# The MLP's second layer norm as a factor per token behind its first product

## The chip, the cores and the metric

The kernel runs on one core of one Trainium2 chip. Its time is the device time of one launch in microseconds (us), as the median over runs: 713.09 us of three runs (712.26 to 713.43). The core has five engines that matter here, each with its own instruction queue that it works through in order: PE (matrix products; PEld is its weight load), DVE (elementwise work and reductions), ACT (functions with scale and bias), POOL (elementwise work, on-chip memory alone) and SP (issues DMAs). Products land in eight PSUM banks, which PE shares out among all its jobs. Every wait is a semaphore, so an instruction that waits holds back all that stands behind it in its queue.

## The reference

```
xn = layernorm(x)                                  # x: 2048 tokens x 512, eps 1e-5, no weights
out = x + A(xn) + B(xn)
A:  q, k, v = xn@wq, xn@wk, xn@wv                  # 32 heads of 16; 4 segments of 512 tokens
    per segment: causal softmax attention, mixed by sigmoid(beta) with
    a linear memory  phi(q)M / (phi(q)z + 1e-6),  phi(t) = t+1 if t>0 else exp(t)
    then M += phi(k)^T v,  z += sum phi(k)
    A = o @ wo
B:  y = layernorm(xn)                              # a second norm of tokens already normalized
    h = gelu(y @ w1 + b1)                          # 512 -> 1792, tanh form
    B = h @ w2 + b2
```

The mean of a normalized token is zero, so the second norm only scales it: y = xn * r with one number r per token, where r = 1/sqrt(v/(v+eps) + eps) for a token of variance v.

## The kernel before

All products but the softmax-weighted sum over V and some small ones are made of two-part f16 numbers: each operand is split into a high and a low half, and three matmuls (high by high, high by low, low by high) stand for one. `split3` (L456 on, its matmul on L465) issues these: 12 matmuls for a 512-long contraction.

Tokens arrive as [128, 512] tiles `xt`. `norm_stats` takes mean and variance on DVE (L397, L398), adds eps, goes through Ln and Exp on ACT, and refines with a Newton step on DVE (L407 to L410). It makes two pairs of factor and offset per token: one for the first norm, one for both norms in one. `norm_apply` applies a pair in place, on POOL (L418). `ln_tr` transposes a normalized tile with four PE transposes (L450), and ACT (L453) and DVE (L454) write its high and low halves.

This is done twice. The kind "X" loads tokens, takes statistics, applies the first pair and fills `xnT`, the transposed tokens of a segment of 512, which feed Q, K and V (`qk_proj`, `v_nat`). The kind "Y" loads the same tokens again, applies the second pair, and fills `yT`, half a segment of 256 tokens, which feeds the MLP. Either has one buffer, which is refilled when its last reader is done.

The MLP runs in 16 units j: half segment j//2, and one half of the 1792 features (7 tiles of 128). Unit j has seven D steps (`d_jobs`): 12 matmuls of 256 columns each into a bank, evicted with scale `CG` and bias `b1t` into `hz`, four of the seven by ACT (L724), three by DVE (L726), as `Z_ON` says. G (`gelu`, L731) is one ACT instruction over all seven, 1792 columns, behind a load of the gelu table; the next exponential loads the other table back (L850). H (`h_split`) splits the result on POOL and ACT (L738 to L740), and e (`e_part`, L764) multiplies by w2 in two accumulator banks. `hz` is the memory of `hT`, two buffers, one for each feature half.

Attention runs in 16 groups i of 8 heads, four for each segment: T makes Q (or K) and sends it through DRAM into stacked form (`qst`, `kst`); M makes the logits once to find row maxima (DVE, L597, with a read of the result after each); R transposes the maxima and sends them through DRAM into `qst`; S makes the logits again and takes exponentials (ACT, L635), with the causal mask on POOL (L644); pv sums over V (L659); O divides (DVE, ACT and POOL); Z, Qd and Q are the memory part; N and K update it; out is the last product (L783). A DVE copy of one number (`fence`, L767) stands in the middle of each MLP unit's second product.

The order of all work is written out in a string, `ORDER`: each letter takes the next step of one of some thirty streams, and all engines get their instructions in that one order. `BANKS` gives the PSUM bank of each product in turn. Fourteen `warm` steps of eight idle matmuls each (L796) can be put anywhere; before, all stand in the start.

Of the kernel before, what the change touches and what calls it, by code (L numbers as in the profile page):

```python
# [9 lines left out]
F32 = mybir.dt.float32  # L10
# [40 lines left out]
Z_ON = "AVAVAVA"  # L51
# [6 lines left out]
def streams():  # L58
# [23 lines left out]
    for n in range(2 * NSEG):  # L82
        again += [("Y", n, 0, 0), ("Y", n, 0, 2), ("Yt", n, 0, 0), ("Yt", n, 0, 1)]
# [21 lines left out]
    "aacttuttcacutvaatcvucuevaatevaacvccvutbcbwtccvtbvvcwfvwtdcvttxxextxvwyxbchxgxxyxoowxoyxowowvyoyzoyzniiibccyygpz"  # L105
    "iiccniipznzyiyfzAnsqpiioiqizzmAqqiwpAzhoAoiiqqzzjpocjiqijjqizjoAjoBAiikskkAkjqiqjqmjjisqjiojiqbiskkkpkibbplafoA"
    "oAjpgjloojqjqjqjlohakkkpkojiqiAajsoijijqjiqjmiAiAifippBkkqqBikipqikoqilBsgaoplahqjjqlqqqjqjoBoijqiajqipamkkkksa"
    "ioojpiqjqiqijqjiaaqjqjsbmqiqBiiBfoikkkbBpkbibpghopoolqqpjqojjjloojiqjqiqilmkpkkkijojiqqqijjqijqiqjqiipkkkpkbiif"
    "mnillnglnnrjjrjqiirpjiqjisqijqikkmkkjijrjjioijioijikkpkkhilmfolomjjbgojqqjpljqjoobsmbkkkkjqqisjqqjijqiqjiqijoiq"
    "iiskkmippqiqpiskaklmiohlfoiqpqaqamqgploooaomjqjqqjqmjqaojpqpsiiqiqoioiqjpqiqiikkkkoapjiqijqijqjpqiqjqsjaqaoihkk"  # L110
    "kkaalmoqjjlbfobqjqjlsqmjgbbqjkkmmkkjqjqmojjjohiojiikkkkipiifplilonnliiiniipmripgnojjmjrjsjorijibkkkpkmiiqjqjqij"
    "qqiijsqiqjohjqiiqpqiipmkpkkskrillfmmlogqqbjjoojqjqjjoomkkpkkiijhooiqjiqjqijqiqpsjiqqjibbpqiqipkkkkliiqaslfoioom"
    "papqqqamgpooasjqqjqjmaoojqjlqjqiqiapqikmkikkiqipoiqjqjaoohijqjaqiqiisopaojiqqjiakmspkkklbopfjqlbqjmjgqjjqqjqlob"
    "bkkkmkmjqjqqiqjqijqjqoimijkpkkkliilfnimiiplgnniipirmoiorponijpjobojjioisjqqjpiiqkkkkiiprijsqsqjiqqjjimqqijrijkk"
    "ipkbsklfloqjqmjglojjqqqjjomsokkkkopjmioiijojqijqipqjqjqiiqqiikppkkkliqlfbbqliqqqimoipmgooojpjqqjojjoomjiikkkpki"
    "qijqijqjqiijqjiqjqiikisqpiskkkqpioqplooplqjjqqjjojjqlopkkkkjqjqqjjojqjoqqpspqkkkkqpqqlqqpqqmpqqqqqqqqqqqmqllqqr"
    "rrr"
# [33 lines left out]
def infini_mixer_kernel(ctx: ExitStack, tc: tile.TileContext, x, wq, wk, wv, wo, beta, w1, b1, w2, b2, out):  # L151
# [68 lines left out]
    def col(j):  # L220
        return sc[:, j:j + 1]
# [166 lines left out]
    stats = cst.tile([P, S // P, 2, 2], F32, name="stats")  # L388

    def norm_stats(tok, tiles):  # L390
# [21 lines left out]
    def norm_apply(tok, tiles, twice, act):  # L412
        for j, t in enumerate(tiles):
            a, b = stats[:, tok + j, twice, 0:1], stats[:, tok + j, twice, 1:2]
# [7 lines left out]
    def ln(kind, n, b, part):  # L422

        tok = 4 * n + 2 * b if kind == "X" else 2 * n
        if part == 0:
            lt[kind, n, b] = ts = []
            for j in range(2):
                name = ("nN", "nD")[j] if (kind, n, b) == ("X", 0, 1) else "xt"
# [3 lines left out]
        elif part == 1:  # L432
            norm_stats(tok, lt[kind, n, b] + (lt[kind, 0, 1] if n == 0 else []))
        else:
            norm_apply(tok, lt[kind, n, b], kind == "Y", (kind, n, b) == ("X", 0, 1))

    def ln_out(kind, n, b, k):
        if kind == "X":
            if n not in xnT:
                xnT[n] = sb.tile([P, KT, 2, SEG], F16, name="xnT")  # L440
# [439 lines left out]
```

## Time and profile before

| | |
|---|---|
| median of 3 runs | 713.09 us (712.26 to 713.43) |
| the profiled execution | 712.69 us, span of its instructions 711.0 us |
| granted TensorE clock | 0.998 |
| PE busy | 693.3 us, 98% |
| PEld busy | 392.6 us, 55% |
| ACT busy | 535.9 us, 75% |
| DVE busy | 531.8 us, 75% |
| POOL busy | 363.7 us, 51% |

The span runs from the first to the last instruction. Busy shares are averages over three stages that differ: a start, in which weights arrive and are split; a long middle, in which attention and MLP units are interleaved; an end, in which no more maxima are to be found and the last unit and group are finished. Matmuls overlap in the pipeline and their ends are modelled, so that PE counts as busy in short waits too. The chain that ended last, followed back from the last instruction, tells in which stage which engine sets the pace.

### The profile page before, as it was taken

What the parts mean: (1) busy time and instruction counts of PE and PEld (TensorE: products, weight loads), DVE (VectorE), ACT (ScalarE), POOL (GpSimd) and SP (SyncE); (2) the same over time, 40 slices, a digit from 0 to 9 for tenths busy, and PEclk for the clock granted to TensorE, in tenths of its full rate; (3) what the DMA queues carried; (4) which work ended last, traced back from release to release, by engine and by line L of the source; (5) the groups of instructions that cost most, each with busy time, mean ns of one, the idle gap of its engine ahead of it and who ended that gap; (6) DMA issues with size and microseconds to landing.
All of it is one profiled execution on the core that took longest, in us unless ns stands there. A gap on an engine that the chain in (4) does not pass through costs nothing.

```text
span 711.0 us, 16718 instructions
## 1 busy us (share of the span) xinstructions
PE 693.3 (98%) x6261; PEld 392.6 (55%) x6261; DVE 531.8 (75%) x1665; ACT 535.9 (75%) x934; POOL 363.7 (51%) x548
## 2 busy tenths in 40 slices
PE   7799999999999999999999999999999999999997
PEld 5464556565654565656554656566545545565542
DVE  5889867979684968978686786979688567978243
ACT  6897898868884678586975777687794768778960
POOL 4675758565632354555624446464724455455652
PEclk9999999999999999999999999999999999999999
DMA  9885233232303124131311412340413215031001
GB/s 288 236 247 152 61 71 96 62 90 74 95 4 103 60 70 113 48 96 42 92 43 57 111 47 77 96 115 2 115 24 103 78 20 146 15 93 19 1 17 59
DMA packets 54093, 59.30 MB, mean 83 GB/s; under 512 B 5038, under 2 KB 40892, under 8 KB 54012
## 3 DMA queue, kind: packets, MB, share of 16 engines
q1 hardware_dynamic: 51708, 54.04, 26.5%
q0 software_dynamic: 2304, 4.20, 3.8%
q8 instruction: 49, 0.80, 0.5%
q14 instruction: 32, 0.26, 0.1%
HBM read 41.18 MB, written 17.04 MB: 82 GB/s over the span
## 4 chain that ended last, share of the span: by engine, by line
PE 67%; DVE 12%; ACT 8%; DMA 6%; POOL 4%; issue 3%; SPq 1%; POOLq 0%; DVEq 0%; ACTq 0%
PE ps L465 26%; PE ps L764 14%; PE ps L659 8%; PE ps L783 6%; PE ps L630 4%; PE ps L590 4%; DVE ps L597 4%; ACT pt L635 3%; DMA kd<-hl 2%; PE ps L450 2%; PE ps L538 1%; DVE hl L485 1%; DMA w1s<-in_B_w_dram 1%; DVE mc L597 1%; DMA pt<-in_A_wv_dram 1%
## 5 line engine op out<-in xcount | busy, mean ns | idle before, releaser
L597 DVE CUSTOM_DVE_ANT_0 ps<-ps,mask 128x512 f32<-128x512 f32 (+3 forms) x512 | 235.0, 524 | 24.1 <-PE ps L590 23.2
L635 ACT ACTIVATE pt<-ps,qkcs 128x512 f32<-128x512 f32 (+1 forms) x384 | 206.9, 628 | 20.2 <-PE ps L630 17.7
L764 PE MATMUL ps<-w2s,hT 64*128 64x512 f16 x1344 | 176.2, 376 | 0.3 <-DVE fence L767 0.2
L465 PE MATMUL ps<-yT,w1s 128*128 128x256 f16 x1344 | 161.2, 273 | 2.5 <-DVE phk L495 1.2
L644 POOL TENSOR_SCALAR_AFFINE_SELECT pt<-pt 128x256 f32<-128x256 f32 x256 | 101.6, 419 | 110.1 <-ACT pt L635 109.2
L465 PEld LDWEIGHTS <-w1s 128*128 128x128 f16 x1344 | 127.2, 98 | 37.4 <-issue 16.9
L764 PEld LDWEIGHTS <-hT 64*128 64x128 f16 x1344 | 70.0, 94 | 57.4 <-issue 9.6
L740 POOL TENSOR_TENSOR hT<-hh,hT 128x512 f16<-128x512 f32 x64 | 66.5, 1039 | 66.7 <-ACT hT L739 65.5
L659 PE MATMUL ps<-pt,vt 128*32 128x512 f32 (+3 forms) x1024 | 77.6, 436 | 0.1
L597 DVE DVE_READ_ACCUMULATOR2_ANT mc<- 128x1 f32 x512 | 72.6, 142 | 0.2
L630 PE MATMUL ps<-qst,kst 50*128 50x512 f16 (+3 forms) x512 | 70.6, 298 | 0.1
L590 PE MATMUL ps<-kst,qst 48*128 48x512 f16 (+3 forms) x512 | 67.2, 298 | 0.7 <-DVE hT L726 0.4
L739 ACT ACTIVATE hT<-hh 128x512 f16<-128x512 f32 x64 | 36.7, 574 | 37.4 <-POOL hh L738 37.2
L738 POOL TENSOR_SCALAR hh<-hT,sc 128x512 f32<-128x512 f32 x64 | 42.6, 666 | 38.5 <-ACT hT L731 37.1
L659 PEld LDWEIGHTS ps<-pt,vt 128*32 128x32 f32 x1024 | 30.6, 109 | 42.0 <-issue 31.4
L724 ACT ACTIVATE hT<-ps,b1t,sc 128x256 f32<-128x256 f32 x64 | 36.6, 571 | 17.1 <-PE ps L465 16.6
L465 PE MATMUL ps<-xnT,wqs 128*128 128x512 f16 x192 | 45.0, 384 | 0.4 <-DVE mc L597 0.4
L783 PE MATMUL ps<-wos,oT 128*128 128x512 f16 x192 | 44.0, 380 | 0.9 <-POOL oT L695 0.6
L465 PE MATMUL ps<-xnT,wks 128*128 128x512 f16 x192 | 44.2, 380 | 0.0
L465 PE MATMUL ps<-wvs,xnT 128*128 128x512 f16 x192 | 43.5, 379 | 0.6 <-DVE hT L726 0.3
L726 DVE TENSOR_SCALAR hT<-ps,sc,b1t 128x256 f32<-128x256 f32 x48 | 25.7, 539 | 24.5 <-PE ps L465 24.4
L590 PEld LDWEIGHTS <-qst 48*128 48x128 f16 x512 | 27.1, 94 | 30.7 <-issue 14.8
(217 smaller groups left out, 958.7 us busy)
## 6 DMA issues: line engine op xcount, KB each, us to landing
xt<-in_A_x_dram SPq DMA_DIRECT2D x30, 256.0 KB
kd<-hl SPq DMA_DIRECT2D x48, 128.0 KB
kst<-kd SPq DMA_DIRECT2D x32, 192.0 KB
qd<-hl SPq DMA_DIRECT2D x48, 128.0 KB
qst<-qd SPq DMA_DIRECT2D x32, 192.0 KB
acc<-in_A_x_dram SPq DMA_DIRECT2D x16, 256.0 KB
acc<-in_B_b_dram POOLq DMA_DIRECT2D x16, 256.0 KB, 4.3
out_dram<-acc SPq DMA_DIRECT2D x16, 256.0 KB
```

The costliest lines, as they stand in the source:

```text
L465: T.matmul(p, wsl(ws, k, a), xsl(xs, k, b), start=s0 and i == 0, stop=s1 and i == 3 * n - 1)
L590: T.matmul(p[:, o:o + n], stk[i, 0][r, t, P * qb:P * qb + P], stk[i, 1][r, t, :n], start=True, stop=True)
L597: V.tensor_tensor_reduce(p[:, o:o + n], p[:, o:o + n], mask[:, 512 - n:], 1.0, -3e38, OP.add, OP.max, mc[i][:, 4 * b + t, qb:qb + 1])
L630: T.matmul(p[:, o:o + n], stk[i, 1][r, t, P * kb:P * kb + P], stk[i, 0][r, t, P * kb:], start=True, stop=True)
L635: A.activation(e[:, OFF[kbs[0]]:OFF[kbs[0]] + o], p[:, :o], AF.Exp, scale=qkcs[:, 1, i % NG:i % NG + 1])
L644: G.affine_select(v, v, pattern=[[0, 2], [1, P]], compare_op=OP.is_ge, fill=0.0, base=0, channel_multiplier=-1)
L659: T.matmul(p[32 * c:32 * c + 32, P * kb:], vt[s, kb][:, 4 * g + c, 16 * odd:16 * odd + 32], pt[i, 2 * c + odd][:, OFF[kb]:OFF[kb] + LEN[kb ...
L738: G.tensor_scalar(t, hz[:, z, :], col(SHH + j % 2), 0.0, op0=OP.mult, op1=OP.add)
L739: A.activation(hT[:, z, 0, :], t, AF.Copy)
L740: G.tensor_tensor(hT[:, z, 1, :], t, hT[:, z, 0, :], op=OP.subtract)
L764: T.matmul(pes[j][a], hTs[fh][r, fi, u, P * a:P * a + P], w2s[r, fo, v, :], start=n == 0 and m == 0, stop=fi == FH - 1 and m == 2, skip_gr ...
L783: T.matmul(p, o[:, u, P * b:P * b + P], wos[:, g, v, :], start=i == 0, stop=i == 3 * NG - 1)
```

## The change

The second norm is no longer made on its own tiles. The MLP's first product reads `xnT`, the half segment that belongs to the unit, and its result is multiplied by the token's ratio at the eviction. Tokens are columns there, so the ratio has to lie along the columns, equal in all 128 partitions: a new step `ratio` multiplies the ratios of a segment by `CG` (DVE, [128, 4]), writes the 512 numbers to DRAM, 4 bytes each at its place, and reads them back into all partitions (`sr0`, `sr1`: 128 x 512, one for each feature half). There are eight such steps. The eviction is now always a `tensor_tensor` on DVE with two inputs, the bank and `sr`; the bias moves into the gelu, which becomes seven instructions of 256 columns with a bias column each. `norm_stats` makes the first pair and the ratio. All of "Y" is gone: 16 loads of tokens, 16 applications on POOL, 64 transposes, 16 evictions each on ACT and DVE.

A new `ORDER` and new `BANKS` go with it. `xnT` still has one buffer, and so all four MLP units of a segment must have read it before the next segment's tokens are transposed into it. One of the fourteen warm steps now stands in the middle, in group 8.

```diff
-Z_ON = "AVAVAVA"
...
-    for n in range(2 * NSEG):
-        again += [("Y", n, 0, 0), ("Y", n, 0, 2), ("Yt", n, 0, 0), ("Yt", n, 0, 1)]
+    again = [("ratio", n, fh) for n in range(NSEG) for fh in range(2)]
...
-    "aacttuttcacutvaatcvucuevaatevaacvccvutbcbwtccvtbvvcwfvwtdcvttxxextxvwyxbchxgxxyxoowxoyxowowvyoyzoyzniiibccyygpz"
+    "cuauctacacavcetttcauvttttaaccccvvcceuvuatttvawwecvfwttdxxxxbvwyxxyxchxgyvxwxoycwwoywxfyyzovnoozoocsziiiiyzppnzg"
...
-        q = r[:, :, :, 0]
         V.tensor_tensor(b, y, y, op=OP.mult)
         V.scalar_tensor_tensor(b, b, -0.5, a, op0=OP.mult, op1=OP.mult)
-        V.scalar_tensor_tensor(q, b, 1.5, y, op0=OP.add, op1=OP.mult)
-        V.scalar_tensor_tensor(r[:, :, :, 1], ag[:, :, 0:1].broadcast_to([P, n, 2]), -1.0, q, op0=OP.mult, op1=OP.mult)
+        V.scalar_tensor_tensor(y, b, 1.5, y, op0=OP.add, op1=OP.mult)
+        V.tensor_copy(r[:, :, 0], y[:, :, 0])
+        V.scalar_tensor_tensor(r[:, :, 1], ag[:, :, 0], -1.0, y[:, :, 0], op0=OP.mult, op1=OP.mult)
+        V.tensor_tensor(a[:, :, 0], a[:, :, 0], y[:, :, 0], op=OP.mult)
+        V.tensor_tensor(rat[:, tok:tok + n], a[:, :, 0], y[:, :, 1], op=OP.mult)
...
+    def ratio(n, fh):
+
+        r = sm.tile([P, 4], F32, name="r4")
+        V.tensor_scalar(r, rat[:, 4 * n:4 * n + 4], col(CG + fh), None, op0=OP.mult)
+        d = dr.tile([1, SEG], F32, name=f"rd{fh}")
+        Q.dma_start(d.rearrange("a (j p) -> p (a j)", p=P), r)
+        srow[n, fh] = sb.tile([P, SEG], F32, name=f"sr{fh}")
+        Q.dma_start(srow[n, fh], d.broadcast_to([P, SEG]))
...
     def d_jobs(j):
         hf, fh = divmod(j, 2)
+        hs, hh = divmod(hf, 2)
+        own = slice(256 * hh, 256 * hh + 256)
...
-                                    (yT[hf], lambda t, k, a: t[:, k, a, :])), KT, True, True)
-                if Z_ON[fi] == "A":
-                    A.activation(hz[:, fi, :], p[:, :256], AF.Identity, bias=b1t[:, fo:fo + 1], scale=col(CG + fh))
-                else:
-                    V.tensor_scalar(hz[:, fi, :], p[:, :256], col(CG + fh), b1t[:, fo:fo + 1], op0=OP.mult, op1=OP.add)
+                                    (xnT[hs], lambda t, k, a: t[:, k, a, own])), KT, True, True)
+                V.tensor_tensor(hz[:, fi, :], p[:, :256], srow[hs, fh][:, own], op=OP.mult)
...
     def gelu(j):
-        A.activation(hzs[j % 2], hzs[j % 2], AF.Gelu_apprx_tanh)
+        for f in range(FH):
+            z = hzs[j % 2][:, f, :]
+            A.activation(z, z, AF.Gelu_apprx_tanh, bias=b1t[:, FH * (j % 2) + f:FH * (j % 2) + f + 1])
```

What the new order moves is shown at three places. The first is DVE's queue in the start, up to the first row maxima. `hT` is the destination of a D eviction, `wvs`, `wqs` and `w2s` are weight splits, `phk` is the K feature of the memory, ISA with `mask` is a maximum and ISA `mc` the read of its result. Before:

```order
L726 TENSOR_SCALAR hT_112<-ps_597,sc,b1t 128x256
L377 SCALAR_TENSOR_TENSOR wvs<-pt,sc,wvs 128x512 x2
L377 SCALAR_TENSOR_TENSOR wqs<-pt,qksc,wqs 128x512
L726 TENSOR_SCALAR hT_112<-ps_634,sc,b1t 128x256
L377 SCALAR_TENSOR_TENSOR w2s<-w2s,sc 128x512
L597 ISA ps_684,mc<-ps_684,mask 128x512
L597 ISA mc 128x1
```

And now:

```order
L490 SCALAR_TENSOR_TENSOR hl<-ps_576,hl 128x512
L499 TENSOR_SCALAR phk<-phk,qksc 128x512
L500 SCALAR_TENSOR_TENSOR phk<-ps_576,phk 128x512
L374 SCALAR_TENSOR_TENSOR w2s<-w2s,sc 128x512
L730 TENSOR_TENSOR hT_113<-ps_607,sr_454 128x256
L730 TENSOR_TENSOR hT_113<-ps_638,sr_454 128x256
L730 TENSOR_TENSOR hT_113<-ps_652,sr_454 128x256
L730 TENSOR_TENSOR hT_113<-ps_667,sr_454 128x256
L730 TENSOR_TENSOR hT_113<-ps_681,sr_454 128x256
L602 ISA ps_700,mc<-ps_700,mask 128x512
L602 ISA mc 128x1
```

Five of unit 0's seven evictions now stand in one piece ahead of the first maximum, with the second K feature ahead of them.

The second place is SP's queue about group 7's maxima (`md`), in the third segment's first units. Before:

```order
L430 DMA xt<-in_A_x_dram 128x512 x2
L744 DMA acc<-in_A_x_dram 128x512
L610 DMA md_98<-mhl 32x2x128
L613 DMA qst_90<-md_98 2x2048 x2
L430 DMA xt<-in_A_x_dram 128x512 x2
L486 DMA kd_93<-hl 8x16x512
```

And now:

```order
L441 DMA xt<-in_A_x_dram 128x512 x2
L750 DMA acc<-in_A_x_dram 128x512
L429 DMA rd_4879<-r_4877 128x4x1
L431 DMA sr_4881<-rd_4879 128x512
L615 DMA md_98<-mhl 32x2x128
L618 DMA qst_90<-md_98 2x2048 x2
L491 DMA kd_93<-hl 8x16x512
```

The ratio's write and its read back stand right ahead of the maxima's way through DRAM; the read waits for the write to land.

The third place is ACT's queue at the end, about the last unit's gelu. Before:

```order
L635 ACTIVATE pt<-ps_9840,qkcs 128x256
L635 ACTIVATE pt<-ps_9841,qkcs 128x256
L724 ACTIVATE hT_113<-ps_9848,b1t,sc 128x256
L731 ACT_TABLE_LOAD
L731 ACTIVATE hT_113<-hT_113 128x1792
L739 ACTIVATE hT_113<-hh 128x2x256 x2
L850 ACT_TABLE_LOAD
L507 ACTIVATE nD<-oT 128x512
```

And now:

```order
L699 ACTIVATE oT<-nN 128x512
L737 ACT_TABLE_LOAD
L737 ACTIVATE hT_114<-hT_114,b1t 128x256 x7
L745 ACTIVATE hT_114<-hh 128x2x256
L672 ACTIVATE nN<-ps_9768,bg 128x512
L673 ACTIVATE nD<-ps_9768,eo 128x512
L855 ACT_TABLE_LOAD
L640 ACTIVATE pt<-ps_9806,qkcs 128x512
L640 ACTIVATE pt<-ps_9807,qkcs 128x512
```

The last gelu stood behind the last exponential (`pt`) of the last group; now twelve exponentials and the group's second half follow it.

More of the change, by code (lines that the diff above doesn't have):

```diff
@@ L386, in infini_mixer_kernel @@
     F1, S1, F2, S2, CG, SHH, C2, B1F = range(5, 21, 2)
-    stats = cst.tile([P, S // P, 2, 2], F32, name="stats")
+    stats = cst.tile([P, S // P, 2], F32, name="stats")
+    rat = cst.tile([P, S // P], F32, name="rat")
     def norm_stats(tok, tiles):
@@ L432, in ln, with ln_out @@
         elif part == 1:
-            norm_stats(tok, lt[kind, n, b] + (lt[kind, 0, 1] if n == 0 else []))
+            norm_stats(tok, lt[n, b] + (lt[0, 1] if n == 0 else []))
         else:
[L435 to L440, printed above, removed]
-            ln_tr(lt["X", n, b][k], xnT[n], 256 * b + P * k)
-        else:
-            if n not in yT:
-                yT[n] = sb.tile([P, KT, 2, 256], F16, name="yT")
-            ln_tr(lt["Y", n, b][k], yT[n], P * k)
+            norm_apply(tok, lt[n, b], (n, b) == (0, 1))
+    def ln_out(n, b, k):
+        if n not in xnT:
+            xnT[n] = sb.tile([P, KT, 2, SEG], F16, name="xnT")
+        ln_tr(lt[n, b][k], xnT[n], 256 * b + P * k)
     def ln_tr(t, dst, c0):
@@ L838, in infini_mixer_kernel @@
         "out": lambda s, b: out_jobs(s)[b](),
[L839 to L840 removed]
+        "X": ln, "Xt": ln_out, "ratio": ratio, "gate": gates,
         "D": lambda j, f: once("D", j, lambda: d_jobs(j))[f](),
```

62 lines of the change are left out of this document (29 added, 33 removed).

## The prediction

> **What bounds the kernel now.** I read the page's totals and the chain that ended last, then the chain stage by stage, then the engines' busy time in the same stages.
>
> ```profile
> span 711.0 us, 16718 instructions
> PE 693.3 (98%) x6261; PEld 392.6 (55%) x6261; DVE 531.8 (75%) x1665; ACT 535.9 (75%) x934; POOL 363.7 (51%) x548
> ...
> PE 67%; DVE 12%; ACT 8%; DMA 6%; POOL 4%; issue 3%; SPq 1%; POOLq 0%; DVEq 0%; ACTq 0%
> ```
>
> PE is busy nearly always, but the chain lies on it for only 67%, 476 us. The chain's lines for 30 to 82 us, for 82 to 646 us, and from there to the end:
>
> ```profile
> by line: DVE ps L597 23.5%; DMA acc<-in_A_x_dram 6.5%; DVE w1s L377 5.9%; DMA kd<-hl 5.5%; POOL w1s L381 5.2%; issue 5.2%; POOL w1s L379 4.8%; DVE w2s L377 4.5%; DVE wqs L377 4.4%; DVE mc L597 4.3%; DVE wvs L377 4.0%; ACT w1s L380 3.7%; DVE
> by line: PE ps L465 32.9%; PE ps L764 18.0%; PE ps L659 10.2%; PE ps L783 5.7%; PE ps L630 5.4%; PE ps L590 5.3%; DVE ps L597 3.0%; PE ps L450 2.0%; issue 1.9%; ACT pt L635 1.8%; PE ps L538 1.4%; DVE hl L485 1.1%; DMA qd<-hl 0.8%; DMA qst<-
> by line: ACT pt L635 13.4%; PE ps L783 12.6%; POOL hT L740 8.6%; issue 6.4%; POOL hh L738 5.7%; ACT hT L731 5.2%; POOL pt L644 4.4%; ACT hT L739 4.4%; ACT L731 3.9%; ACT L850 3.9%; POOL nN L691 3.9%; POOL nN L689 3.9%; DVE oT L513 2.5%; ACT
> ```
>
> In the start the DVE lines alone make 46.6%, 24 of 52 us: DVE paces it. In the middle PE's make 80.9%. The end goes through ACT and POOL. How full the engines are in the middle:
>
> ```profile
> 82.00:250.00 168.00, 167.67 (x1588) 94.62 (x1590) 130.59 (x436) 132.92 (x236) 88.50 (x140) 1.00 0.26 69
> 250.00:450.00 200.00, 199.33 (x1884) 115.02 (x1880) 154.04 (x482) 152.92 (x265) 97.27 (x151) 1.00 0.29 75
> 450.00:646.00 196.00, 195.42 (x1766) 108.97 (x1760) 152.40 (x469) 145.50 (x252) 97.26 (x148) 1.00 0.26 68
> ```
>
> The columns behind the length are PE, PEld, DVE, ACT and POOL. DVE is busy for 437 of 564 us (77%), ACT for 431 (76%). So PE work that goes is worth its length in the middle, and work that moves to DVE is the question.
>
> **The change part by part.** The sum is made against the profiled execution: 712.69 us, of which 711.0 is span; the median of the runs is 0.4 above it.
>
> *Transposes.* Of 64 that go, 8 lie in the start, where DVE paces: nothing. In the middle L450 had, in two windows and in a piece of the chain:
>
> ```profile
> 82.00:250.00 168.00, 4.58 (x32) 3.62 (x32) 1.00 0.26 69
> 250.00:450.00 200.00, 5.52 (x40) 4.44 (x40) 1.00 0.29 75
> 450.00:646.00 196.00, 4.55 (x32) 3.62 (x32) 1.00 0.26 68
> ...
> 333.75 1.02 PE ps L450 x8
> ```
>
> 104 stand there; 48 are X's (four for each of segments 1 to 3's twelve tiles), so 56 go. Eight take 1.02 us on the chain: 7.1 us. The chain's 2.0% of 564 is 11.3 us for 104: 6.1. I take 6.6 off. All D matmuls stay.
>
> *The warm step.* Eight matmuls of 256 columns move out of the start, where they cost nothing, into the middle. Twelve such take 1.42 us in a piece of the chain (82.30, below): 1.0 us more, unless PE would wait there anyway.
>
> *Evictions and gelu.* The rows:
>
> ```profile
> 82.30 1.42 PE ps L465 x12
> ...
> L597 DVE CUSTOM_DVE_ANT_0 ps<-ps,mask 128x512 f32<-128x512 f32 (+3 forms) x512 | 235.0, 524 | 24.1 <-PE ps L590 23.2
> L724 ACT ACTIVATE hT<-ps,b1t,sc 128x256 f32<-128x256 f32 x64 | 36.6, 571 | 17.1 <-PE ps L465 16.6
> L726 DVE TENSOR_SCALAR hT<-ps,sc,b1t 128x256 f32<-128x256 f32 x48 | 25.7, 539 | 24.5 <-PE ps L465 24.4
> L512 DVE TENSOR_TENSOR oT<-oT,nD 128x512 f32<-128x512 f32 x16 | 11.4, 714 | 4.5 <-ACT nD L508 4.4
> L574 DVE TENSOR_TENSOR mst<-ps,mst 128x48 f32<-128x48 f32 x8 | 1.6, 204 | 1.6 <-PE ps L569 1.6
> L454 DVE SCALAR_TENSOR_TENSOR yT<-ps,yT 128x512 f16<-128x512 f32 x16 | 10.5, 680 | 4.0 <-ACT yT L453 4.0
> L453 ACT ACTIVATE yT<-ps 128x512 f16<-128x512 f32 x16 | 8.9, 588 | 0.2 <-PE ps L450 0.2
> L731 ACT ACTIVATE hT<-hT 128x1792 f32<-128x1792 f32 x16 | 27.2, 1697 | 0.2
> L739 ACT ACTIVATE hT<-hh 128x256 f16<-128x256 f32 x16 | 6.7, 417 | 4.7 <-POOL hh L738 4.5
> L376 ACT ACTIVATE w1s<-w1s,sc 128x512 f16<-128x512 f32 x5 | 3.6, 713 | 0.0
> L380 ACT ACTIVATE w1s<-w1s 128x512 f16<-128x512 f32 x7 | 4.4, 627 | 1.8 <-POOL w1s L379 1.7
> L325 DVE TENSOR_SCALAR sc<-sc 128x1 f32<-128x1 f32 x8 | 1.2, 154 | 0.3
> ```
>
> No DVE product of a bank with a second tensor at 256 columns is in the trace: between 204 ns (48 columns) and 714 (512), by a line 0.43. I take 0.54, since the nearest row, the present eviction L726, reads the same bank and writes the same tile. In the middle lies 564/711 of the work: 51 of 64 evictions move, +27.5 us on DVE; 14 yT halves go, -9.5; three more small operations of about 0.15 for each of six statistics, and six ratios, +3.6. DVE has 21.6 us more there. On ACT 51 evictions go (-29.1) and 14 yT halves (-8.2). A gelu piece is L739's 0.42 plus what a column operand adds (0.713 - 0.627): 0.50, seven of them 3.5 instead of 1.70, for 13 units +23.4. ACT has 13.9 us less.
>
> How much of it reaches the end? DVE's chain is 12% of 711, 85 us; less the 24 of the start it is at most 61 in the middle, 14% of DVE's 437. Taken in proportion, +3.0 us; both ends are 0, if all fits in DVE's free 127 us, and 21.6, if every bit stands in PE's way. ACT in the same way: 8% is 57 us, of which the listed ACT lines of the end are 30.8% of 65, 20; 37 of 431 is 9%: -1.3.
>
> The Trainium skill ("ScalarE: Activation LUTs", section "What ACT_TABLE_LOAD costs") gives an ACTIVATE with a column bias 280 ns plus 0.833 per column, and lets neighbours overlap by 93: by that a gelu piece is estimated at 0.40, ACT has 23 us less instead of 14, and the sum would be 0.8 lower. The trace's only gelu row is without bias.
>
> *The start.* Unit 0's four further evictions are 2.2 us on DVE, less one yT half (0.68) that fell behind the weights; the statistics and ratio add some 0.5: +2. Ends: 0, if the relieved ACT lets DVE's inputs come earlier, and 4, if unit 1's four count too. The two token loads that leave the queues there make room for the same amount of w1 that now stands ahead of the first K: nothing.
>
> *POOL and SP.* 16 applications leave POOL at no gain, since it is 51% busy. The ratio's two DMAs on SP are costed at nothing because of DVE rows that stand between a ratio and the first eviction that needs it: in segment 1 eight maxima (235.0/512 each, 3.7 us, without their reads), two accumulator adds, two halves of xnT. What it costs without that cover is the second rival.
>
> *The end.* Its chain before:
>
> ```profile
> 670.00 5.82 ACT pt L635 x12
> ...
> 676.56 1.28 ACT L731
> 677.85 1.71 ACT hT L731
> ...
> 690.40 0.15 DVE fence L767
> 690.58 0.70 DVE rc L512
> ...
> 694.35 1.28 POOL nN L689
> 695.69 1.27 POOL nN L691
> ...
> 698.91 8.17 PE ps L783 x37
> ```
>
> The last exponential ends at 676; then the last table, gelu and split run to 690, the fence of the last unit holds the division's Newton steps on DVE, and out starts at 698.9: 22.8 us. Now the gelu stands ahead of the last twelve exponentials. Behind them remain the mask, pv, the division (690.58 to 698.9, 8.3 us) and its Ln and Exp (some 3): about 11, so 12 less. Ahead of them ACT has two table loads, seven pieces and copies more: 2.6 + 3.5 + about 2 = 8. Net -4; ends -1, if ACT falls behind, and -6, if pieces overlap.
>
> *Sum:* -6.6 + 1.0 + 3.0 - 1.3 + 2 - 4 = -5.9; 712.7 - 5.9 = 706.8, said as 707.
>
> **The rivals.**
>
> *DVE takes over (slower).* Place: the bursts in which a segment's last unit must be read out of xnT before the next tokens, seven evictions in a row that ACT shared before, with maxima and PSUM releases queued behind. For: DVE goes from 77% to 81% of the middle, and the K and Q features wait in the same queue. Against: its chain share in the middle is small. It decides once more than 8.9 of the 21.6 us (3.0 and the 5.9 of the gain) land on the chain; with two thirds, 14.4, the time is 707 - 3 + 14.4, 718.
>
> *The ratio's way through DRAM shows (slower).* SP waits in order, and group maxima stand behind it:
>
> ```profile
> 65.23 2.87 DMA kd<-hl
> ...
> 349.40 4.37 DMA qd<-hl
> ...
> 252.07 1.41 DMA md<-mhl
> ```
>
> Two transfers are 2.8 to 8.7 us by these, and 512 pieces of 4 bytes are finer than any of them; the cover is some 6. With 3 us bare in three segments, 9 us: 716. The Trainium skill ("DMA: Bandwidth & Descriptors", section "Specifications") asks for 512 B and more at line rate, with read-modify-write below; it gives no time for this shape, and no run here shows one.
>
> *No change.* The transposes filled waits of PE that stay: without the 6.6 it is 713.4. The Trainium skill speaks for it: matmul busy is a bad measure of nearness to the limit, LDWEIGHTS busy a good one ("Perfetto Trace Analysis", section "Identifying the Most-Contended Engine"). PEld's 55% agrees with that rule; the chain's 81% on PE in the middle, measured by what released what, speaks for work.
>
> **How the numbers follow.** The forecast has 0.56, DVE 0.22, the ratio 0.10, no change 0.12. About 0.2%, 1.4 us, is what a measurement can tell from none. So faster 0.56, same 0.12, slower 0.32. The likeliest case alone lies between 700 (transposes 7.1, end -6, no DVE term, start 0) and 711. For 8 in 10 the upper end has to take in the ratio's 716 and most of DVE's: 700 to 718.
>
> **What would show it.** Right: L450 has 64 fewer matmuls and the chain in the middle stays on PE; DVE is near 550 us busy, ACT near 515; unit 15's gelu ends before the last exponential, and out starts some 12 us after that exponential. Wrong: waits of PE or ACT for the new eviction of some us each, more chain on DVE than 85 us, DMA of `rd` or `sr` on the chain, the new eviction far over 0.54, or PE waiting for the token transposes at a segment's border.

## The result, and the profile after

The changed kernel is slower: 758.55 us in the median of four runs (757.42 to 759.25) beside 712.67 for the kernel before (712.18 to 713.43), a ratio of 1.0638 with a 95% interval of 1.0619 to 1.0657. That is 45.9 us more, far outside the range of 700 to 718. The profiled execution took 759.22 us.

The page of the changed kernel, its totals, the granted clock in 40 slices (in tenths), and the chain that ended last by engine and by line:

```profile
span 757.2 us, 16667 instructions
PE 702.2 (93%) x6197; PEld 401.0 (53%) x6197; DVE 540.6 (71%) x1742; ACT 516.8 (68%) x950; POOL 352.2 (47%) x532
...
PEclk9899799999899999999899999999979999999999
...
PE 57%; DMA 13%; DVE 11%; ACT 9%; issue 4%; POOL 4%; SPq 1%; POOLq 0%; DVEq 0%; ACTq 0%
PE ps L470 23%; PE ps L770 12%; PE ps L664 7%; PE ps L635 4%; PE ps L789 4%; DMA rd<-r 4%; PE ps L595 4%; DVE ps L602 3%; DMA md<-mhl 2%; ACT pt L640 2%; DMA sr<-rd 2%; DMA kd<-hl 2%; DMA qd<-hl 1%; PE ps L543 1%; DMA w2s<-in_B_w_dram 1%
```

PE fell from 98% to 93%. DVE and ACT are less busy as a share than before, so neither has become the bound. What grew is DMA on the chain, from 6% to 13%, and the new names there are `rd<-r`, the write of the ratio, `sr<-rd`, its read, and `md<-mhl`, the maxima. The engines' sum over 82 to 646 us, the middle, shows how much PE lost there:

```profile
sum 564.00, PE 530.04 PEld 298.32 DVE 413.20 ACT 385.58 POOL 252.24; mean PE 176.68 PEld 99.44 DVE 137.73 ACT 128.53 POOL 84.08
```

PE was idle for 34.0 of 564 us; before it was 1.6. Over the whole span its idle time grew from 17.7 to 55.0 us, and its busy time by 8.9 us although it has 64 matmuls fewer: matmuls at half clock, shown below, take longer. The waits, and the groups of the new eviction and the new gelu:

```profile
DVE hT L730 <- DMA sr<-rd: 28.8, 5, 7.7
PE ps L635 <- DMA qst<-md: 10.1, 3, 7.5
PE ps L470 <- DVE hT L730: 7.0, 1, 7.0
PE ps L595 <- DVE hT L730: 6.8, 1, 6.8
```

```profile
L730 DVE TENSOR_TENSOR hT<-ps,sr 128x256 f32<-128x256 f32 x112 | 44.6, 420 | 54.2 <-DMA sr<-rd 28.8
L737 ACT ACTIVATE hT<-hT,b1t 128x256 f32<-128x256 f32 x112 | 46.5, 496 | 0.2
```

DVE stands still for up to 7.7 us at the first eviction of a unit until its row `sr` has landed, and PE waits for a bank that DVE has not released, or for the maxima. One such place is segment 1's first unit. The chain from 176 to 200 us, in order of time, and SP's issues there:

```profile
179.99 0.16 DVE r L427
180.16 10.51 DMA rd<-r
190.69 3.16 DMA sr<-rd
...
193.97 0.44 DVE hT L730
194.41 0.05 issue
194.46 4.61 PE ps L470 x12
```

```profile
180.16 0.38 SPq L429 DMA_DIRECT2D rd<-r  x1
190.69 0.33 SPq L431 DMA_DIRECT2D sr<-rd  x1
191.06 0.42 SPq L615 DMA_DIRECT2D md<-mhl  x1
194.03 0.54 SPq L618 DMA_DIRECT2D qst<-md  x2
```

The write takes 10.5 us from its issue until the read may be issued. SP waits for it, and the maxima stand behind the read and are issued at 191.06. In all eight trips this time is 7.9 to 11.6 us; of the six later ones the mean is 10.2. With the 3.2 that the read takes here a trip is 13 to 14 us long. The same place in windows (the columns behind the length are PE, PEld, DVE, ACT and POOL busy, then the granted clock):

```profile
178.00:187.40 9.40, 9.40 (x93) 6.38 (x87) 7.69 (x32) 7.93 (x18) 5.94 (x9) 1.00 0.05 1
187.40:194.50 7.10, 0.09 (x3) 0.05 (x2) 0.53 (x2) 2.90 (x6) 2.22 (x5) 0.78 0.16 39
194.50:198.20 3.70, 3.70 (x9) 1.29 (x10) 0.89 (x2) 0.00 (x0) 0.00 (x0) 0.50 0.02 7
```

PE stops for 7 us, and when it starts again the clock granted to it is half.

### The profile page after: what moved, and what is told of

The parts are those of the page before. It is cut to its first block, busy times and chain, and to the rows that moved or that the text cites. A ratio compares the mean times of both kernels' runs of the same rounds, so it can differ in the third digit from the quotient of the medians.

```text
span 757.2 us, 16667 instructions
## 1 busy us (share of the span) xinstructions
PE 702.2 (93%) x6197; PEld 401.0 (53%) x6197; DVE 540.6 (71%) x1742; ACT 516.8 (68%) x950; POOL 352.2 (47%) x532
## 4 chain that ended last, share of the span: by engine, by line
PE 57%; DMA 13%; DVE 11%; ACT 9%; issue 4%; POOL 4%; SPq 1%; POOLq 0%; DVEq 0%; ACTq 0%
PE ps L470 23%; PE ps L770 12%; PE ps L664 7%; PE ps L635 4%; PE ps L789 4%; DMA rd<-r 4%; PE ps L595 4%; DVE ps L602 3%; DMA md<-mhl 2%; ACT pt L640 2%; DMA sr<-rd 2%; DMA kd<-hl 2%; DMA qd<-hl 1%; PE ps L543 1%; DMA w2s<-in_B_w_dram 1%
## 5 line engine op out<-in xcount | busy, mean ns | idle before, releaser
L470 PE MATMUL ps<-xnT,w1s 128*128 128x256 f16 x1344 | 161.3, 276 | 0.5 <-DVE mc L602 0.3
L470 PEld LDWEIGHTS <-w1s 128*128 128x128 f16 x1344 | 130.3, 99 | 30.3 <-issue 10.4
L770 PEld LDWEIGHTS <-hT 64*128 64x128 f16 x1344 | 74.3, 94 | 57.8 <-issue 9.7
L730 DVE TENSOR_TENSOR hT<-ps,sr 128x256 f32<-128x256 f32 x112 | 44.6, 420 | 54.2 <-DMA sr<-rd 28.8
L635 PE MATMUL ps<-qst,kst 50*128 50x512 f16 (+3 forms) x512 | 73.1, 299 | 10.8 <-DMA qst<-md 10.1
L664 PE MATMUL ps<-pt,vt 128*32 128x256 f32 (+3 forms) x1024 | 78.0, 436 | 0.0
L490 DVE SCALAR_TENSOR_TENSOR hl<-ps,hl 128x512 f16<-128x512 f32 x32 | 22.1, 690 | 46.4 <-ACT phq L489 22.9
L470 PE MATMUL ps<-xnT,wqs 128*128 128x512 f16 x192 | 48.7, 407 | 7.0 <-DVE hT L730 7.0
L470 PE MATMUL ps<-xnT,wks 128*128 128x512 f16 x192 | 48.1, 402 | 7.5 <-DVE xnT L460 4.3
L635 PEld LDWEIGHTS <-kst 50*128 50x128 f16 x512 | 28.3, 94 | 41.2 <-issue 12.8
```

What stands on the lines that cost most here:

```text
L470: T.matmul(p, wsl(ws, k, a), xsl(xs, k, b), start=s0 and i == 0, stop=s1 and i == 3 * n - 1)
L635: T.matmul(p[:, o:o + n], stk[i, 1][r, t, P * kb:P * kb + P], stk[i, 0][r, t, P * kb:], start=True, stop=True)
L664: T.matmul(p[32 * c:32 * c + 32, P * kb:], vt[s, kb][:, 4 * g + c, 16 * odd:16 * odd + 32], pt[i, 2 * c + odd][:, OFF[kb]:OFF[kb] + LEN[kb ...
L730: V.tensor_tensor(hz[:, fi, :], p[:, :256], srow[hs, fh][:, own], op=OP.mult)
L770: T.matmul(pes[j][a], hTs[fh][r, fi, u, P * a:P * a + P], w2s[r, fo, v, :], start=n == 0 and m == 0, stop=fi == FH - 1 and m == 2, skip_gr ...
```

## The experiments

Theory A, formed on these rows: the write of the ratio in 512 pieces of 4 bytes is so slow that it holds SP (and the maxima behind it) and DVE (in order, with all banks that it must release); PE's gaps follow from both. Theory B: DVE's added work. Theory C: the new order, in which Q, K, V and the MLP share `xnT`. The first four kernels were timed together, beside 712.84 us of the kernel before.

**Larger pieces.** On the changed kernel:

```diff
-        Q.dma_start(d.rearrange("a (j p) -> p (a j)", p=P), r)
+        Q.dma_start(d.rearrange("a (p j) -> p (a j)", j=4), r)
...
-                V.tensor_tensor(hz[:, fi, :], p[:, :256], srow[hs, fh][:, own], op=OP.mult)
+                V.tensor_tensor(hz[:, fi, :].rearrange("p (j c) -> p j c", j=2), p[:, :256].rearrange("p (j c) -> p j c", j=2),
+                                srow[hs, fh].rearrange("p (c j) -> p j c", j=4)[:, 2 * hh:2 * hh + 2, :], op=OP.mult)
```

> The ratio is written in 128 pieces of 16 bytes instead of 512 of 4 (token p of tile j at place 4p+j), read back whole, and the eviction reads it with a stride of four numbers. Theory A (the write of many small pieces holds SP's queue, and DVE behind it; PE's gaps of 3 to 7.5 us follow, and after them the clock at half): from rd<-r's issue to sr<-rd's 2 to 3 us instead of 7.9 to 11.6; PE's gaps over 3 us in the middle go (34 us together), and the half clock behind them (37 us at half, 18 us of time): 758.5 - 34 - 18 = 706, with some of the gaps left 706 to 722. Theory B (DVE's added load): unchanged, over 750. Theory C (the order, and xnT shared by Q, K, V and the MLP): over 740. If a write through DRAM takes 8 us whatever its pieces are: over 750 too, with rd<-r as long as before.

It took 715.66 us, 1.0039 (1.0020 to 1.0058) of the kernel before. The later six trips now have 1.4 to 3.4 us between write and read instead of 8.5 to 11.6; SP's issues of the one above:

```profile
169.60 0.33 SPq L429 DMA_DIRECT2D rd<-r  x1
171.00 0.33 SPq L431 DMA_DIRECT2D sr<-rd  x1
```

No gap of PE in the middle reaches 0.9 us. Of the 45.9 us, 42.9 are gone with the same order and more DVE work (an eviction takes 619 ns in this kernel), so B and C are not the cause.

**No trip, or a trip that only holds SP.** Both leave the multiplication in place:

```diff
+        if n:                                  # e2_no_trip
+            srow[n, fh] = srow[0, fh]
+            return
         r = sm.tile([P, 4], F32, name="r4")
...
-        srow[n, fh] = sb.tile([P, SEG], F32, name=f"sr{fh}")
-        Q.dma_start(srow[n, fh], d.broadcast_to([P, SEG]))
+        t = sb.tile([P, SEG], F32, name=f"sr{fh if n == 0 else 1}")      # e3_hold
+        srow[n, fh] = srow[0, 0] if n else t
+        Q.dma_start(t, d.broadcast_to([P, SEG]))
```

> The two transfers of the ratio are made for segment 0 alone; segments 1 to 3 multiply by segment 0's row, so their outputs leave out their own factor. All DVE work of the eviction stays. A: 704 to 712, with no PE gap over 3 us in the middle that ends on DVE hT or on md, and a granted clock of 0.99. B: over 745, since DVE's work is the same. C: over 735.

> The transfers of segments 1 to 3 are made as in the changed kernel (512 pieces of 4 bytes, then the read), but into a tile that nobody reads, and the evictions multiply by segment 0's first row: the factor is left out, and DVE no longer waits for sr. SP is held as long as before. If A's damage comes through DVE's wait for sr (28.8 us of waits in five places): 712 to 722. If it comes through SP (maxima and K features queued behind, 10.1 us of PE waits for qst<-md): 735 to 750. I expect a mixture nearer to the first, 725. B: over 745.

Without the later trips it is 717.61 us, 1.0065 (1.0043 to 1.0088), over the 704 to 712 that I expected; segment 0's two long trips are still in it. With trips that nobody waits for on DVE it is 746.76, 1.0473 (1.0438 to 1.0508). So the trips cost 29.2 us through SP and its queue alone, and I had put it the other way round, with most of the damage in DVE's wait. DVE's wait on top adds 11.8.

**The same hold in the kernel before.** Six idle trips ahead of maxima:

```diff
+    def trip():
+        d = dr.tile([1, SEG], F32, name="rd")
+        Q.dma_start(d.rearrange("a (j p) -> p (a j)", p=P), b1t[:, :4])
+        t = sb.tile([P, 40], F32, name="idle")
+        Q.dma_start(t, d[:, :t.shape[1]].broadcast_to([P, t.shape[1]]))
...
-        "M": lambda i, n: once("M", i, lambda: m_jobs(i))[n](),
+        "M": lambda i, n: (trip() if n == 8 and i in (3, 4, 7, 8, 11, 12) else None, once("M", i, lambda: m_jobs(i))[n]()),
```

> The kernel before, and six idle trips of the same kind (128 x 4 numbers in 512 pieces of 4 bytes to DRAM, then a read of it that nobody uses) on SP ahead of the maxima of groups 3, 4, 7, 8, 11 and 12, after eight of their twelve jobs. A: SP is held 8 to 11 us six times; with some 6 us of cover in the maxima jobs, PE waits some 3 us in three of them and the clock falls behind these: 720 to 735. B and C: 713, since DVE's work and order are those of before.

722.11 us, 1.0142 (1.0113 to 1.0170): 9.3 us more, with the trips holding SP for 7.0 to 11.3 us each and one new PE gap over 3 us (3.58, at 184). The cause works in the old order too, and costs less there. The two are not quite alike: the idle read here has 40 columns instead of 512, and the trips stand at other places.

**The clock behind a gap.** Idle matmuls in two gaps of the changed kernel:

```diff
+    def fill(bank, n):
+        p = dps.tile([P, 512], F32, name=f"ps{bank}", bufs=1)
+        w = ones.bitcast(F16)
+        for _ in range(n):
+            T.matmul(p[:, :256], w[:, :P], w, start=True, stop=True)
...
+        "T": lambda i, w: (fill(7, 48) if (i, w) == (4, 0) else None, qk_proj(i, w)),
+        "S": lambda i, t, n: (fill(2, 56) if (i, t, n) == (11, 0, 0) else None, once("S", i, lambda: s_jobs(i))[t][n]()),
```

> The changed kernel with all its trips and waits, and idle matmuls (128x256, read by nobody) in two of the gaps: 48 ahead of the first Q product of group 4, in the gap of 7.01 us at 187.4, and 56 ahead of the first S product of group 11, in that of 7.54 us at 546.2. At 0.107 us each they fill 5.1 and 6.0 us. If the half clock behind a gap costs time of its own, the stretches of 6.8 us (from 191.4) and 10.2 us (from 549.8) at half clock go and with them up to 3.4 + 5.1 us: 750 to 755 instead of 758.5. If the clock's fall is without consequence: 758.5, or a little more for the idle work.

757.27 us, 1.0624 (1.0608 to 1.0639): the interval overlaps that of the changed kernel, so as a time it decides nothing. Locally it shows what was meant. The first filled gap, and the stretch behind it:

```profile
188.50:194.70 6.20, 5.75 (x56) 4.88 (x51) 0.00 (x0) 3.15 (x6) 2.40 (x6) 1.00 0.11 36
...
196.30:203.00 6.70, 6.70 (x62) 3.29 (x62) 3.61 (x6) 2.99 (x6) 1.16 (x1) 1.00 0.18 54
```

The clock stays at 1.00, and from the last maximum of group 3 to that of group 4 it is 54.3 us instead of 55.8, from group 11's to group 12's 53.7 instead of 55.3. So the half clock costs about 1.5 us behind a gap of 7 us; half of the stretches at half clock, 3.4 and 5.1, would have been the loss if PE had been the limit there. The Trainium skill ("TensorE: Matmul & The Clock Gate", section "What's actually happening") has half the clock after an idle window of about 3.4 us and the full one after a busy window of as long, and the stretches seen, 3.4, 6.8 and 10.2 us, agree with it; a gap shorter than that window was enough in some places, however (last section). Its account of what that costs (section "HAM oscillation — how this bites in real kernels") is half of the throttled time, which is two to three times what was measured here.

**A repaired version.** From the first two experiments together: one trip per segment in 16-byte pieces, and one copy that puts the row in the order of the tokens, so that the eviction need not stride.

```diff
-        r = sm.tile([P, 4], F32, name="r4")
-        V.tensor_scalar(r, rat[:, 4 * n:4 * n + 4], col(CG + fh), None, op0=OP.mult)
-        d = dr.tile([1, SEG], F32, name=f"rd{fh}")
-        Q.dma_start(d.rearrange("a (j p) -> p (a j)", p=P), r)
-        srow[n, fh] = sb.tile([P, SEG], F32, name=f"sr{fh}")
-        Q.dma_start(srow[n, fh], d.broadcast_to([P, SEG]))
+        if fh:
+            return
+        d = dr.tile([1, SEG], F32, name="rd")
+        Q.dma_start(d.rearrange("a (p j) -> p (a j)", j=4), rat[:, 4 * n:4 * n + 4])
+        raw = sb.tile([P, SEG], F32, name="raw")
+        Q.dma_start(raw, d.broadcast_to([P, SEG]))
+        srow[n] = raw
+
+    def straight(n):
+        t = sb.tile([P, SEG], F32, name="sr")
+        V.tensor_copy(t.rearrange("p (j c) -> p j c", j=4), srow[n].rearrange("p (c j) -> p j c", j=4))
+        srow[n] = t
...
-                V.tensor_tensor(hz[:, fi, :], p[:, :256], srow[hs, fh][:, own], op=OP.mult)
+                if j % 4 == 0 and fi == 0:
+                    straight(hs)
+                V.scalar_tensor_tensor(hz[:, fi, :], p[:, :256], col(CG + fh), srow[hs][:, own], op0=OP.mult, op1=OP.mult)
```

> One trip per segment instead of two, in 128 pieces of 16 bytes; a single copy on DVE per segment brings the row into the order of the tokens, so that the eviction reads it in a row again, and the eviction applies the weight's factor (a power of two) itself. Four permuting copies of some 0.9 us in place of 112 evictions that took 0.20 us longer in e1_16B: 19 us less on DVE. From the stretches of the earlier runs: e1_16B's 173.3 to the maxima of group 3 and e2_no_trip's 534.3 behind it are 707.6, plus up to 3 for the copies: 708 to 711 for the execution that is profiled. If DVE's load does not matter (my share of one seventh on the chain): 3 us under e1_16B, 712. If something else in the new order costs, as much as e1_16B: 715.

710.82 us beside 712.95, 0.9968 (0.9956 to 0.9981). It beats both kernels: the idea of the change is worth 2.1 us once the trip is short, and this version is 47.7 us under the changed kernel. The four copies and the evictions of this kernel:

```profile
L436 DVE COPY sr<-raw 128x512 f32<-128x512 f32 x4 | 4.1, 1030 | 0.0
...
L738 DVE SCALAR_TENSOR_TENSOR hT<-ps,sc,sr 128x256 f32<-128x256 f32 x112 | 51.0, 477 | 22.0 <-PE ps L476 18.0
```

**What the transposes are worth.** Into the repaired version, 56 idle transposes:

```diff
+                if fi == 0 and fh == 0 and hf:
+                    for k in range(8):
+                        T.transpose(p[:, P * (k % 4):P * (k % 4) + P], ident, ident)
                 split3(p[:, :256], ((WT["1"], lambda w, k, a: w[:, fo, a, P * k:P * k + P]),
```

> e6_one_trip with eight idle 128x128 transposes ahead of the first product of each of the seven later hidden halves, as many as the second norm's transposes that the change took out of the middle; nobody reads them. If transposes are worth their length on PE, as the sum has it: 6.6 to 7.1 over e6_one_trip. If they filled waits that stay (the rival of no change): 0 to 2 over it.

715.32 us, 1.0030 (1.0020 to 1.0041), 4.5 over the repaired version, between the two expectations. They show 7.4 us of PE, so some 60% of their length reaches the end, at places that are not those of the transposes taken out:

```profile
L736 PE MATMUL ps<-ident 128*128 128x128 f32 x56 | 7.4, 275 | 0.0
```

**Which pieces are slow.** Twelve idle trips in the kernel before, two of each shape; c is the number of columns, e the numbers per piece, gap the spacing:

```diff
+    SHAPES = [(1, 1, 1), (2, 1, 1), (4, 1, 1), (1, 4, 1), (4, 2, 1), (4, 1, 16)]
+    def trip(i):
+        c, e, gap = SHAPES[i % 6]
+        d = dr.tile([1, c * P * e * gap], F32, name=f"rd{i % 6}")
+        to = d.rearrange("a (c p e) -> p (a c) e", p=P, c=c)[:, :, :e]
+        Q.dma_start(to, b1t[:, :c * e].rearrange("p (c e) -> p c e", c=c))
+        t = sb.tile([P, 1], F32, name="idle")
+        Q.dma_start(t, d[:, :1].broadcast_to([P, 1]))
```

> The kernel before with twelve idle trips on SP, ahead of the maxima of groups 2 to 13, of six shapes in turn, each followed by a read that waits for it: 128, 256 and 512 pieces of 4 bytes, 128 of 16, 512 of 8, and 512 of 4 bytes with 64 bytes between their starts. The time from the write's issue to the read's issue: if the number of pieces sets it, 128x4 as 128x16 (1.4 to 3.4 us), 256x4 halfway, 512x8 as 512x4 (7 to 11 us), whatever the distance. If pieces that share a line of DRAM set it, 512 with 64 bytes between them are about as quick as 128, and 128x4 stands over 128x16.

SP's issues, write and read, of one trip per shape: 128 pieces of 16 bytes (at 173.73), 512 of 8 (194.81), 512 of 4 with 64 bytes between their starts (252.95), 128 of 4 (275.98), 512 of 4 (380.67).

```profile
173.73 0.42 SPq L609 DMA_DIRECT2D rd<-b1t  x1
176.46 0.33 SPq L611 DMA_DIRECT2D idle<-rd  x1
194.81 0.44 SPq L609 DMA_DIRECT2D rd<-b1t  x1
199.17 0.34 SPq L611 DMA_DIRECT2D idle<-rd  x1
252.95 0.44 SPq L609 DMA_DIRECT2D rd<-b1t  x1
255.21 0.33 SPq L611 DMA_DIRECT2D idle<-rd  x1
275.98 0.44 SPq L609 DMA_DIRECT2D rd<-b1t  x1
284.28 0.32 SPq L611 DMA_DIRECT2D idle<-rd  x1
...
380.67 0.45 SPq L609 DMA_DIRECT2D rd<-b1t  x1
389.08 0.34 SPq L611 DMA_DIRECT2D idle<-rd  x1
```

| pieces | in 64 bytes | us from write to read, both trips |
|---|---|---|
| 512 of 4 B, 64 B apart | 1 | 2.3, 3.2 |
| 128 of 16 B | 4 | 2.7, 3.5 |
| 512 of 8 B | 8 | 4.4, 6.0 |
| 128 of 4 B | 16 | 8.3, 7.4 |
| 256 of 4 B | 16 | 7.8, 8.5 |
| 512 of 4 B | 16 | 8.4, 8.4 |

The number of pieces does nothing: 128 take as long as 512. What counts is how densely they lie: from one piece in 64 bytes to sixteen the mean goes from 2.7 to 8.1 us, some 0.36 us for each further one. That 64 bytes is the stretch that matters is not shown, since no other distance was tried. My theory had the wrong half of "many small pieces". As a whole kernel this one was run once, at 724.30 us.

**The same in the changed kernel.** As e3_hold, with a short read, the 512 pieces side by side or 64 bytes apart:

```diff
+        if n:
+            srow[n, fh] = srow[0, fh]
+            d = dr.tile([1, SEG * 16], F32, name="far")      # e9_near: SEG * 1, e=1
+            Q.dma_start(d.rearrange("a (j p e) -> p (a j) e", p=P, e=16)[:, :, 0], r)
+            Q.dma_start(sm.tile([P, 1], F32, name="idle", bufs=1), d[:, :1].broadcast_to([P, 1]))
+            return
```

> As e3_hold, but the read behind each write of segments 1 to 3 is of one number per partition: the evictions multiply by segment 0's row (the later segments' own factor is left out), and only SP is held, for the landing of 512 adjacent pieces of 4 bytes. It is the partner of e10_far. If the hold alone made e3_hold's 746.8: 740 to 747. If the read of 512 columns had a part in it: 725 to 735.

> As e9_near, with 64 bytes between the starts of the 512 pieces instead of 4, and nothing else changed. e8_shapes gave 2.3 and 3.2 us for that shape and 8.4 for the adjacent one. If pieces that share 64 bytes of DRAM are the cause: SP is free after 2 to 3 us, and the time is e2_no_trip's 717.6 plus 0 to 3. If 512 pieces of 4 bytes are dear as such: as e9_near.

Beside 712.29 us of the kernel before: 737.77, 1.0351 (1.0336 to 1.0367) side by side, and 718.06, 1.0077 (1.0062 to 1.0091) apart. The first of the later trips of each on SP, near and far:

```profile
177.03 0.38 SPq L432 DMA_DIRECT2D far<-r  x1
187.37 0.33 SPq L433 DMA_DIRECT2D idle<-far  x1
187.75 0.42 SPq L621 DMA_DIRECT2D md<-mhl  x1
```

```profile
178.76 0.38 SPq L432 DMA_DIRECT2D far<-r  x1
180.68 0.33 SPq L433 DMA_DIRECT2D idle<-far  x1
185.01 0.33 SPq L621 DMA_DIRECT2D md<-mhl  x1
```

10.3 us against 1.9 with the same 512 pieces of 4 bytes. The DMA engines are not what takes longer: in both traces the records of this write's packets end 1.3 us after its issue. The sixteen marks by which SP learns of the landing come 7.3 to 10.3 us after the issue in e9_near, and 1.6 to 1.9 in e10_far. Far apart, the trips cost what none cost (717.61). The near one is 9.0 us under e3_hold, below the range that I gave for the hold alone and just over the one for the read having a part: the read of 512 columns ahead of the maxima has a part, about a third of the 29.2.

**The read later on SP.** In the changed kernel with its full trips:

```diff
-        Q.dma_start(srow[n, fh], d.broadcast_to([P, SEG]))
+        back[n, fh] = lambda: Q.dma_start(srow[n, fh], d.broadcast_to([P, SEG]))
+        if n == 0 or (n, fh) == (2, 0):
+            back[n, fh]()
+
+    back = {}
+    LATER = {("R", 3): (1, 0), ("R", 4): (1, 1), ("R", 11): (3, 0), ("R", 12): (3, 1), ("D", 9, 0): (2, 1)}
```

> The changed kernel with the full trips, but in five of the six later ones the read of sr is issued behind the maxima's transfers (of groups 3, 4, 11 and 12) or right ahead of the unit that needs it, so that SP does not stand still between the write and the read; DVE still waits for sr. If SP's hold makes the damage (29 us between e3_hold and e2_no_trip): 730 to 735. If DVE's wait does it just as well once SP is free, since sr comes no earlier: 745 to 755.

751.83 us, 1.0569 (1.0535 to 1.0602): only 6.7 less than the changed kernel, although SP was free in five trips. DVE's wait for `sr` is still 27.4 us in five places. And SP was free, but its queue was not. Three transfers that SP issued behind a write that had not landed stand on the chain:

```profile
185.59 4.17 DMA md<-mhl
...
234.59 8.58 DMA kd<-hl
...
540.48 8.76 DMA md<-mhl
```

In e2_no_trip, without the writes, the same three take 1.4, 3.0 and 2.7 us from the last issue to the transfer that waits for them. So this run does not take the first wait away: the slow write holds what is issued behind it, whether SP stands still or not. 11.8 us come back without DVE's wait, 6.7 with SP free, 40.9 without both the writes and the wait (e2_no_trip).

**DVE's load.** The repaired version without its copies, so that the eviction strides over the row (which now has two buffers in turn, `raw0` and `raw1`):

```diff
-                if j % 4 == 0 and fi == 0:
-                    straight(hs)
-                V.scalar_tensor_tensor(hz[:, fi, :], p[:, :256], col(CG + fh), srow[hs][:, own], op0=OP.mult, op1=OP.mult)
+                V.scalar_tensor_tensor(hz[:, fi, :].rearrange("p (j c) -> p j c", j=2),
+                                       p[:, :256].rearrange("p (j c) -> p j c", j=2), col(CG + fh),
+                                       srow[hs].rearrange("p (c j) -> p j c", j=4)[:, 2 * hh:2 * hh + 2, :], op0=OP.mult, op1=OP.mult)
```

> e6_one_trip without the permuting copy: the eviction reads the row with a stride of four numbers, as in e1_16B, which took 0.62 us instead of 0.42, so that DVE has 22 us more evictions and 4 us less copies; the trips stay at one per segment. If DVE's load reaches the end by its share of the chain, one seventh: 2.5 to 3 over e6_one_trip, 713.5. If the difference of 4.8 us between e1_16B and e6_one_trip was all DVE's: 715.6. If it was the four trips saved: 711.

716.68 us, 1.0060 (1.0037 to 1.0083), above all three expectations. The evictions are 73.3 us instead of 51.0, less 4.1 of copies, 18.2 more on DVE:

```profile
L736 DVE SCALAR_TENSOR_TENSOR hT<-ps,sc,raw 128x256 f32<-128x256 f32 x112 | 73.3, 678 | 17.0 <-PE ps L476 13.7
```

5.9 us of these 18.2 reach the end (by the ratios to the kernel before 6.5, give or take 1.9): about a third. A seventh would be 2.6.

**DVE relieved at ACT's cost.** What was still open was whether that third also comes back.

```diff
-                V.scalar_tensor_tensor(hz[:, fi, :], p[:, :256], col(CG + fh), srow[hs][:, own], op0=OP.mult, op1=OP.mult)
+                V.tensor_tensor(hz[:, fi, :], p[:, :256], srow[hs][:, own], op=OP.mult)
...
-            A.activation(z, z, AF.Gelu_apprx_tanh, bias=b1t[:, FH * (j % 2) + f:FH * (j % 2) + f + 1])
+            A.activation(z, z, AF.Gelu_apprx_tanh, bias=b1t[:, FH * (j % 2) + f:FH * (j % 2) + f + 1], scale=col(CG + j % 2))
```

> e6_one_trip with the weight's factor moved from the eviction to the gelu, as its scale column: the eviction is a plain product again (0.42 instead of 0.48 us, 112 times: 6.4 us less on DVE), and the gelu pieces take a second column operand on ACT. At the slope that e12_stride showed (5.9 us of time for 18.2 of DVE): 2.1 under e6_one_trip, 708.7. If ACT's pieces grow by 0.05 or more and ACT is as near to the chain as DVE: as e6_one_trip or above, 710.8 to 712. At the prediction's one seventh: 709.9.

711.45 us, 0.9974 (0.9963 to 0.9986), not to be told from the repaired version. DVE's evictions fell by 6.6 us, ACT's gelu pieces rose from 495 to 588 ns, 10.3 us in all, so that the two may balance. What ACT's share is by itself, none of the runs shows.

## Why the prediction was wrong

- **The ratio's two DMAs, costed at nothing: the step that failed.** The cover named, some 6 us of DVE rows, is there: of a trip of 13.7 us DVE waits for 7.7 at most. But the trip is 13 to 14 us, not the 2.8 to 8.7 that other transfers gave. With the measured 10.2 and 3.2, less the same 6, six trips are 44 us, beside the 40.9 that they cost (758.55 less the 717.61 of e2_no_trip). That the sum comes so near is in part luck: it has one wait per trip, and the runs show two, 29.2 us through SP and its queue and 11.8 through DVE. The second rival named this mechanism and SP's order with the maxima; it put 3 us bare in three segments and 716, and gave it 0.10. Its size was off, and the nearest rows have other pieces: 64 of 256 bytes for `md<-mhl`. The Trainium skill ("DMA: Bandwidth & Descriptors", section "Specifications"), cited there, has a read-modify-write below 512 B; the slow shape would fit it, but the 512 pieces of 4 bytes apart, as far below, took 1.8 to 3.4 us, so that the size alone tells nothing here.
- **Transposes, -6.6.** 64 matmuls are gone; put back as 56 they cost 4.5. The sign was right, the size too high: the length on PE is right (7.4 against 7.1), and less of it reaches the end.
- **DVE, +3.0.** Near by luck, as two errors cancel. The eviction was 0.42 us and not the 0.54 taken: the nearest row in form was the wrong one, the line between two products of tensors (0.43) the right one. DVE is busy for 540.6 us and not some 550. But about a third and not a seventh of added work reached the end in the one experiment on it; a third of the 8.8 us added is 2.9.
- **ACT, -1.3.** A gelu piece takes 0.496 us beside 0.50 predicted, but neighbours overlap, which the sum left out: 112 pieces keep ACT busy for 46.5 us, 0.42 each, near the 0.40 that the prediction set beside its sum. ACT is busy for 516.8 us beside 515. Its share of the end is open (last experiment).
- **The start, +2.** In the repaired version PE did 67.1 us of work in the first 82 instead of 71.5; eight transposes (1.0) and eight warm matmuls (0.9) are not due there, so PE is 2.4 behind. In the changed kernel segment 0's two long trips add their part, which the prediction does not have: the last maximum of group 1 starts at 106.6 us in e2_no_trip, which keeps them, and at 97.6 in the repaired version, and of these 9.0 us 8.3 are left at the last maximum of group 15.
- **The end, -4.** From the last exponentials to out it was to be some 12 us instead of 22.8 (by its rows 23.1):

```profile
731.40 2.62 PE ps L664 x28
...
744.92 8.17 PE ps L789 x37
```

The last exponential ends at 731.5 us and out starts at 744.9, 13.4 later. From the last maxima to the end it is 53.9 us instead of 57.6.

- **The warm step, +1.0,** was not tried by itself. DVE as the new bound and no change at all, the other rivals, did not come: DVE is at 71%, and at 78% in the repaired version, which is faster than the kernel before.

So without the long trip the forecast has the right sign and is too large: 2.1 us gained by the repaired version instead of 5.9. That version has 4.1 us of copies and 6.4 of slower evictions more on DVE; if a third of them reaches the end, they are 3.5 us of the difference, which no run shows by itself.

## What to carry to other kernels

Before a small tensor goes through DRAM, look at how its pieces lie there: numbers of 4 bytes from different partitions side by side land late, and a layout with each partition's numbers together, or 64 bytes from the others', was 2.6 to 5.6 times as quick here. Such a write costs its landing to everything behind it on its queue, to the read that waits for it, and to every engine in order behind the reader. When two waits share one cause, take away the cause; taking away one wait shows little.

## What the runs showed of the hardware that was not expected

- A DRAM write of 128 to 512 pieces of 4 bytes side by side takes 7.0 to 11.6 us until a read of it may be issued, 512 pieces 64 bytes apart 1.8 to 3.4, 128 pieces of 16 bytes 1.4 to 3.5. In the two traces compared above, side by side and apart, the packets' own records end 1.3 us after the issue, so the difference lies behind the DMA engines. That the pieces are read, changed and written back one after another would explain it; the runs do not show it.
- Transfers issued on the same queue behind such a write are late too: in e11_later 4.2 to 8.8 us instead of the 1.4 to 3.0 of e2_no_trip.
- A DVE product of a bank and a row at 128x256 takes 420 ns with the row read in order and 619 with a stride of 16 bytes; with a scalar factor 477 and 678. The Trainium skill ("SBUF — State Buffer", section "Door 1: The DMA port swizzle (why `[64,N]` ≈ `[32,N]`)") has lines of 16 bytes there and a penalty for each access that goes to a new one, and these numbers agree.
- After each PE gap of 3 us or more in the middle the granted clock is at 0.50 for 3.4 to 10.2 us. Of shorter single gaps, five were followed by 3.4 us at half clock (2.9 and 2.8 us in e3_hold, 2.2 in e9_near, 1.8 in e5_fill, 1.5 in e8_shapes), and others by none (2.6 in e5_fill, 2.3 in e3_hold, 2.1 in the changed kernel, 1.9 in e4_before_trip), so the length alone does not decide.
